# One ring of two-bank PSUM tiles, three score chunks a visit, and an exemption between readers of bank 0 and writers of bank 1

## The chip, the cores and the metric

One core of one Trainium2 chip. The metric is the device time of one execution in microseconds. Each comparison uses executions in the fast state only, timed on the same chip in the same rounds as the kernel before; an execution in the slow state (one of e1 below, at 629 us) is left out. The granted clock is the share of TensorE's full clock that the profile records as given to it. Each core has eight PSUM banks, the buffers that matmuls write and ScalarE and VectorE read.

## The reference

```python
scores = scale * np.matmul(q, k.transpose(0, 1, 3, 2)) - np.log(S)   # 8 batches, 12 heads, S=448, D=64
attn = 1.0 / (1.0 + np.exp(-scores))                                 # a sigmoid, no softmax
x = np.matmul(attn, v)            # -> (3584, 768)
g = x @ w_gate                    # 768 x 1536
out = (g * sigmoid(g) * (x @ w_val)) @ w_out                         # 1536 x 768
```

So there are two matrix chains: attention in 64-wide heads, and a gated feed-forward block with 128x128 matmuls.

## The kernel before

Attention works on 24 groups `n` of four heads, three groups to a batch. Each group has seven score "chunks" of four 64x64 matmuls, one sigmoid on ScalarE for a chunk, and a "pv" of 28 matmuls. The first batch's attention runs alone. All the later attention is woven into the feed-forward stream in **visits**: TensorE leaves its 128x128 matmuls, does two score chunks, sometimes a pv, and goes back.

```python
psA = ctx.enter_context(tc.tile_pool(name="psA", bufs=2, space=bass.MemoryType.PSUM))  # scores: 2 x 2 banks
psG = ctx.enter_context(tc.tile_pool(name="psG", bufs=4, space=bass.MemoryType.PSUM))  # the rest: 4 x 1 bank
...
def trans_pe(n, which):                      # q or k of one group
    t = q16.pop((n, which))
    ps = psG.tile([128, C, 128], BF16, tag="G", name="ps_tr")
    for c in range(C):
        nc.tensor.transpose(out=ps[:, c, :], in_=t[:, c].rearrange(...), identity=idn)
    d = qkT.tile([128, C, 128], BF16, tag=f"T{which}", ...)
    nc.vector.tensor_copy(out=d, in_=ps)
...
def ffn1(b, f, gate):                        # one gate or one value group
    ps = psG.tile([128, S], FP32, tag="G", name="ps_g" if gate else "ps_vl")
    for pr in range(NP):
        nc.tensor.matmul(out=ps, lhsT=w[:, pr, cs], rhs=xT[(b, pr)], ...)
    if gate:
        nc.scalar.activation(out=s16, in_=ps, func=SIGM)
        nc.vector.tensor_tensor(out=t1, in0=ps, in1=s16, op=MULT)
    else:
        nc.vector.scalar_tensor_tensor(out=hT[...], in0=ps, scalar=HSC, in1=gcur[0], op0=MULT, op1=MULT)
...
visits = [tiles[i:i + 2] for i in range(0, len(tiles), 2)]
def attn_step(group, pvs):
    scs = [(n, c, qk_tile(n, c)) for n, c in group]
    for n in pvs:
        pv(n)
    for n, c, sc in scs:
        sig_tile(n, c, sc)
```

## Time and profile before

| | before |
|---|---|
| time, median of 3 | 449.12 us (449.05 to 449.71) |
| span of the profiled execution | 446.4 us |
| TensorE busy | 420.9 us, 94% |
| VectorE, ScalarE busy | 49%, 47% |
| mean granted TensorE clock | 0.992 |

With one engine at 94% of the span, the first guess is that it bounds the kernel. The view that tests this is not the busy table but who made TensorE wait, and then where inside its stream time goes that isn't matmuls. The prediction below shows those lines.

### The profile page before, as it was taken

The page shows a single profiled execution, that of the slowest core. Times are in us where ns is not written, and L with a number is a line of the kernel's source. Part 1 is how long each engine was busy: PE and PEld are TensorE (multiplying, and loading weights), DVE is VectorE, ACT ScalarE, POOL GpSimd, SP SyncE. Part 2 cuts the span into 40 slices and gives each one's busy share as a digit, 9 for nine tenths or more (in the row PEclk, how much of TensorE's full clock was granted, in tenths as well). Part 3 has the DMA queues.
Part 4 walks back from the last instruction along what each step waited for, and adds up shares of the span by engine and source line. Part 5 has one row for each costly group of instructions (what it writes and reads, how often), then busy time and mean ns, then how long its engine had stood idle before and what let it go on. Part 6 is the DMA issues. An engine that isn't in the chain of part 4 may idle for free.

```text
span 446.4 us, 7870 instructions
## 1 busy us (share of the span) xinstructions
PE 420.9 (94%) x3252; PEld 212.2 (48%) x3252; DVE 220.1 (49%) x360; ACT 210.9 (47%) x267; POOL 100.7 (23%) x142
## 2 busy tenths in 40 slices
PE   2678999999999999999999999999999999999992
PEld 1344444444555444444555444444555545555661
DVE  1265665466334456556424546646524446555231
ACT  3887675655533655565444464565444441221000
POOL 1764140220234512000324612200021100000221
PEclk9899999999999999999999999999999999999998
DMA  8999999994284986500278694220033300000242
GB/s 264 332 286 286 182 249 196 232 280 149 58 249 94 262 248 167 164 1 1 50 222 231 135 302 134 42 42 3 0 82 87 79 4 1 1 1 0 72 106 70
DMA packets 63587, 59.88 MB, mean 134 GB/s; under 512 B 35648, under 2 KB 61760, under 8 KB 63552
## 3 DMA queue, kind: packets, MB, share of 16 engines
q1 hardware_dynamic: 52992, 41.30, 34.8%
q0 software_dynamic: 10560, 18.09, 19.3%
q8 instruction: 25, 0.41, 0.4%
q14 instruction: 10, 0.08, 0.1%
HBM read 47.19 MB, written 11.01 MB: 130 GB/s over the span
## 4 chain that ended last, share of the span: by engine, by line
PE 92%; ACT 2%; DMA 2%; DVE 1%; issue 1%; POOL 0%; SPq 0%; POOLq 0%; ACTq 0%
PE ps_o L213 25%; PE ps_vl L186 25%; PE ps_g L186 25%; PE ps_sc L137 9%; PE ps_pv L160 7%; ACT pt L148 2%; DMA st<-in_q_dram 2%; PE ps_tr L120 1%; DVE xT L170 1%; SPq L88 0%; POOL c L108 0%; DVE osb L220 0%; POOL out_dram L228 0%; POOLq L391 0%; ACTq L148 0%
## 5 line engine op out<-in xcount | busy, mean ns | idle before, releaser
L148 ACT ACTIVATE pt<-ps_sc,sb_t 128x896 f16<-128x896 f32 x168 | 159.6, 1005 | 88.5 <-PE ps_sc L137 88.5
L186 PE MATMUL ps_g<-xT,wg 128*128 128x448 f16 x576 | 125.4, 353 | 1.5 <-DVE xT L170 1.4
L186 PE MATMUL ps_vl<-xT,wv 128*128 128x448 f16 x576 | 124.9, 353 | 0.0
L213 PE MATMUL ps_o<-wo,hT 128*128 128x384 f16 x672 | 113.5, 326 | 0.0
L193 DVE TENSOR_TENSOR t<-ps_g,s 128x448 f16<-128x448 f32 x96 | 59.9, 624 | 84.7 <-ACT s L191 84.1
L191 ACT ACTIVATE s<-ps_g 128x448 f16<-128x448 f32 x96 | 52.2, 544 | 103.2 <-PE ps_g L186 103.2
L213 PEld LDWEIGHTS <-hT 128*128 128x128 f16 x672 | 64.0, 98 | 48.6 <-issue 7.9
L186 PEld LDWEIGHTS <-wv 128*128 128x128 f16 x576 | 54.3, 98 | 58.6 <-issue 10.7
L186 PEld LDWEIGHTS <-wg 128*128 128x128 f16 x576 | 54.1, 98 | 57.0 <-issue 9.7
L228 POOL DMA_DIRECT2D out_dram<-osb x56 | 29.3, 528 | 211.2 <-DVE osb L220 211.0
L170 DVE CAST xT<-ps_pv 64x448 f16<-64x448 f32 x96 | 59.7, 622 | 30.8 <-PE ps_pv L160 29.4
L198 DVE SCALAR_TENSOR_TENSOR hT<-ps_vl,t 128x448 f16<-128x448 f32 x96 | 60.0, 625 | 16.6 <-PE ps_vl L186 8.5
L220 DVE TENSOR_SCALAR osb<-ps_o 128x384 f32<-128x384 f32 x56 | 31.2, 558 | 74.6 <-PE ps_o L213 74.4
L137 PE MATMUL ps_sc<-T,T 64*64 64x448 bf16 x672 | 51.1, 370 | 8.8 <-ACT pt L148 7.2
L108 POOL CAST c<-st 128x896 bf16<-128x896 f32 x43 | 39.7, 939 | 54.7 <-DMA st<-in_q_dram 30.3
L108 POOL CAST v<-st 128x896 f16<-128x896 f32 x24 | 22.6, 942 | 72.8 <-PE ps_pv L160 52.9
L160 PE MATMUL ps_pv<-pt,v 64*64 64x448 f16 x672 | 37.5, 359 | 0.3 <-ACT pt L148 0.3
L137 PEld LDWEIGHTS <-T 64*64 64x64 bf16 x672 | 13.7, 106 | 39.7 <-issue 37.1
L160 PEld LDWEIGHTS <-v 64*64 64x64 f16 x672 | 20.8, 109 | 12.8 <-issue 0.9
L120 PE MATMUL ps_tr<-idn,c 128*128 128x128 bf16 x84 | 7.3, 250 | 6.5 <-DVE c L108 4.7
L120 PEld LDWEIGHTS <-c 128*128 128x128 bf16 x84 | 5.9, 113 | 8.8 <-DVE c L108 4.7
L124 DVE COPY T<-ps_tr 128x896 bf16<-128x896 bf16 x12 | 7.1, 620 | 5.4 <-PE ps_tr L120 5.2
(14 smaller groups left out, 17.2 us busy)
## 6 DMA issues: line engine op xcount, KB each, us to landing
st<-in_q_dram SPq DMA_DIRECT2D x24, 448.0 KB, 4.5
st<-in_k_dram SPq DMA_DIRECT2D x24, 448.0 KB, 5.9
st<-in_v_dram SPq DMA_DIRECT2D x24, 448.0 KB, 7.3
out_dram<-osb POOLq DMA_DIRECT2D x56, 192.0 KB, 3.1
wg<-in_moe_w_gate_dram POOLq DMA_DIRECT2D x4, 576.0 KB, 24.8
wv<-in_moe_w_val_dram POOLq DMA_DIRECT2D x4, 576.0 KB, 29.7
wo<-in_moe_w_out_dram POOLq DMA_DIRECT2D x4, 576.0 KB, 35.4
T<-c SPq DMA_TRANSPOSE x36, 3.2
```

The lines of the kernel that those rows point to most:

```text
L108: eng.tensor_copy(out=o, in_=i)
L137: nc.tensor.matmul(out=sc[w * 64:(w + 1) * 64, h2, :S], lhsT=kt[r, c, w * 64:(w + 1) * 64], rhs=qt[r, :, w * 64:(w + 1) * 64], start=True, ...
L148: nc.scalar.activation(out=pt, in_=sc[:, :, :S], func=SIGM, bias=sb_t, scale=qkscale)
L160: nc.tensor.matmul(out=P[w][h2 * 64:(h2 + 1) * 64, :], lhsT=vt[r, h2, c * D:(c + 1) * D], rhs=pt[r, h2, :], start=(c == 0), stop=(c == C - 1),
L170: nc.vector.tensor_copy(out=x[w * 64:(w + 1) * 64, :], in_=P[w][h2 * 64:(h2 + 1) * 64, :])
L186: nc.tensor.matmul(out=ps, lhsT=w[:, pr, cs], rhs=xT[(b, pr)], start=(pr == 0), stop=(pr == NP - 1))
L191: nc.scalar.activation(out=s16, in_=ps, func=SIGM)
L193: nc.vector.tensor_tensor(out=t1, in0=ps, in1=s16, op=MULT)
L198: nc.vector.scalar_tensor_tensor(out=hT[(b // 2, f)][:, b % 2, :], in0=ps, scalar=HSC, in1=gcur[0], op0=MULT, op1=MULT)
L213: nc.tensor.matmul(out=o, lhsT=lhsT, rhs=wo16[f // FW][:, f % FW, half * hw:(half + 1) * hw], start=(f == 0), stop=(f == NF - 1),)
L220: nc.vector.tensor_scalar(out=osb[:, half * hw:(half + 1) * hw], in0=o, scalar1=HREC, scalar2=None, op0=MULT)
L228: nc.gpsimd.dma_start(out=dst, in_=osb[i * 64:(i + 1) * 64, :])
```

## The change

The eight PSUM banks become one pool of four two-bank tiles that everything shares: a gate and its value group together ("G"), a score chunk, a pv, the transposes of q and k together, and an output pair. A visit takes three chunks, with the pv between the second and the third. The aim is fewer changes between the two forms of matmul, 128x128 and 64x64. Since gate and value now share a tile, the readers of the gate's bank are declared independent of the matmuls that write the value's bank: `declare_no_dep` tells the language that no wait is needed between them (an exemption). The output pair has the same for its first half.

```diff
-    psA = ctx.enter_context(tc.tile_pool(name="psA", bufs=2, space=bass.MemoryType.PSUM))
-    psG = ctx.enter_context(tc.tile_pool(name="psG", bufs=4, space=bass.MemoryType.PSUM))
+    psD = ctx.enter_context(tc.tile_pool(name="psD", bufs=4, space=bass.MemoryType.PSUM))
...
+    def trans_pe(n):
+        ps = psD.tile([128, 2, 8, 128], BF16, tag="D", name="ps_tr")
+        for which in range(2):
+            t = q16.pop((n, which))
+            for c in range(C):
+                nc.tensor.transpose(out=ps[:, which, c, :], ...)
+            d = qkT.tile([128, C, 128], BF16, tag=f"T{which}", name=f"T{which}_{n}")
+            nc.vector.tensor_copy(out=d, in_=ps[:, which, :C, :])
...
+    def ffn1(b, f):
+        D = psD.tile([128, 2, 512], FP32, tag="D", name="ps_gv")
+        key = f"bank1_{b}_{f}"
+        for i, w16 in enumerate((wg16, wv16)):
+            for pr in range(NP):
+                mm = nc.tensor.matmul(out=D[:, i, :S], ...)
+                if i == 1:
+                    tc.add_to_no_dep_group(key, mm.ins)
+        sg = nc.scalar.activation(out=s16, in_=D[:, 0, :S], func=SIGM)
+        tc.declare_no_dep(sg.ins, group=key, reason="reads bank 0; the group writes bank 1")
+        tm = nc.vector.tensor_tensor(out=t1, in0=D[:, 0, :S], in1=s16, op=MULT)
+        tc.declare_no_dep(tm.ins, group=key, reason="reads bank 0; the group writes bank 1")
+        nc.vector.scalar_tensor_tensor(out=hT[...], in0=D[:, 1, :S], scalar=HSC, in1=t1, ...)
...                                         # the output pair: the same, for its first half
-    visits = [tiles[i:i + 2] for i in range(0, len(tiles), 2)]
+    visits = [tiles[i:i + 3] for i in range(0, len(tiles), 3)]
...
-        scs = [(n, c, qk_tile(n, c)) for n, c in group]
+        scs = [(n, c, qk_tile(n, c)) for n, c in group[:2]]
         for n in pvs:
             pv(n)
+        scs += [(n, c, qk_tile(n, c)) for n, c in group[2:]]
```

## The prediction

> **What bounds the kernel now.** I read the page's busy shares first, then who waited for whom on TensorE, then the timeline of one stretch. The page:
>
> ```profile
> PE 420.9 (94%) x3252; PEld 212.2 (48%) x3252; DVE 220.1 (49%) x360; ACT 210.9 (47%) x267; POOL 100.7 (23%) x142
> ```
>
> TensorE is busy for 94% of the span; the next engine is at half. All waits of TensorE from 40 us to the end are these:
>
> ```profile
> core 0 of [0], span 446.4 us
> PE ps_g L186 <- DVE xT L170: 0.5, 1, 0.5
> ```
>
> One wait of half a microsecond in 406 us. So after the first 40 us the kernel is as long as its matmul stream, and a change of buffers can gain there only what lies inside that stream. The timeline of TensorE (start, duration, line, tile, count) shows what does:
>
> ```profile
> 203.27 0.57 PE L137 MATMUL ps_sc<-T,T 64*64 64x448 bf16 x8
> 203.67 1.49 PE L160 MATMUL ps_pv<-pt,v 64*64 64x448 f16 x28
> 205.10 1.31 PE L186 MATMUL ps_vl<-xT,wv 128*128 128x448 f16 x6
> 206.24 1.30 PE L186 MATMUL ps_g<-xT,wg 128*128 128x448 f16 x6
> ...
> 208.51 1.30 PE L186 MATMUL ps_g<-xT,wg 128*128 128x448 f16 x6
> 209.74 0.57 PE L137 MATMUL ps_sc<-T,T 64*64 64x448 bf16 x8
> 210.25 1.31 PE L186 MATMUL ps_vl<-xT,wv 128*128 128x448 f16 x6
> ```
>
> Durations overlap (the pipeline), so take start to start. Six 128x128 matmuls take 206.24 - 205.10 = 1.14 us. If score matmuls follow, they begin 209.74 - 208.51 = 1.23 us after, so going from the 128x128 to the 64x64 form costs about 0.095. Two score chunks before the attention-times-V matmuls ("pv") take 0.40, so 0.20 a chunk; before 128x128 matmuls they take 0.51, so going back costs 0.11. **One visit to the scores thus costs 0.205 us beside its work**, and pv takes 1.33 of work.
>
> The sum closes: 192 groups of six x 1.135 = 217.9; 56 output groups x 1.95 = 109.2; 147 chunks x 0.20 = 29.4; 21 pv x 1.33 = 27.9; 74 visits x 0.205 = 15.2; about 1.6 of transposes: 401 us. From the start of the steady stream at 37.2 to the end of the last matmul at 438.1 the timeline shows 401.
>
> The first 35 us are different. There ScalarE's 21 sigmoids of 0.9 us set the pace, and it is starved around each pv:
>
> ```profile
> 22.52 0.46 PE L137 MATMUL ps_sc<-T,T 64*64 64x448 bf16 x4
> 22.81 2.53 DVE L170 CAST xT<-ps_pv 64x448 f16<-64x448 f32 x4 [6.37 <-PE ps_pv L160]
> 22.91 0.95 PE L120 MATMUL ps_tr<-idn,c 128*128 128x128 bf16 x14
> 23.09 1.01 ACT L148 ACTIVATE pt<-ps_sc,sb_t 128x896 f16<-128x896 f32 x1 [1.76 <-PE ps_sc L137]
> ...
> 25.37 1.16 DVE L124 COPY T<-ps_tr 128x896 bf16<-128x896 bf16 x2
> ```
>
> Here the 14 transposes run while VectorE still casts pv's result; the two copies of them come after, and TensorE doesn't wait. The brackets of ScalarE's idle time between 11 and 35 us add up to 4 us.
>
> **What the Trainium skill says.** "TensorEngine Tiling (Array Packing)", Key Properties: "Mode switching requires drain". The 0.095 + 0.11 us above agrees. "PSUM — Partial Sum Buffer", PSUM bank collisions raise a hardware error: two engines collide only in the same bank and quadrant; different banks run clean. So reading bank 0 while bank 1 is written is sound; no run yet shows it here. "Trainium Kernel Development and Optimization", Best Practices: consistent bubbles can mean that SBUF or PSUM ran out. The kernel before has no such bubbles, and I expect them after.
>
> **The change part by part.**
>
> *Fewer visits.* 147 chunks in threes are 49 visits instead of 74. 25 x 0.205 = **-5.1 us**, all on TensorE's path. No matmul goes away: The counts of groups, chunks and pv stay the same in the new loops. ScalarE and VectorE do the same instructions.
>
> *The ring.* Before, a gate or value group took one of four single banks and scores had their own two pairs, so no group waited. Now a gate-and-value pair ("G", 2.27 us of matmuls), a chunk, a pv, a transpose tile and an output pair each take one of four slots in order, and each waits for the readers of the fourth before it. When three chunks lie between two G, **the second G waits for the first G's last reader**. How late is that? An undisturbed chain in the kernel before:
>
> ```profile
> 363.64 1.30 PE L186 MATMUL ps_g<-xT,wg 128*128 128x448 f16 x6
> 364.77 1.30 PE L186 MATMUL ps_vl<-xT,wv 128*128 128x448 f16 x6
> 364.97 0.54 ACT L191 ACTIVATE s<-ps_g 128x448 f16<-128x448 f32 x1 [1.25 <-PE ps_g L186]
> 365.55 0.62 DVE L193 TENSOR_TENSOR t<-ps_g,s 128x448 f16<-128x448 f32 x1 [1.08 <-ACT s L191]
> 366.27 0.62 DVE L198 SCALAR_TENSOR_TENSOR hT<-ps_vl,t 128x448 f16<-128x448 f32 x1
> ```
>
> The last reader ends 366.89 - 363.64 = 3.25 us after the start, and TensorE sees it some 0.06 later (the gap from the T copy to the first score matmul at 9.11): 3.31. TensorE is ready for the next G after 1.14 + 1.23 + 3 x 0.20 + 0.11 = 3.08. So each such place costs 0.24 us, more where ScalarE or VectorE is behind. I wrote out the order in which the new loops emit their work and counted: 18 visits without a pv stand between two G, and one between a G and a transpose tile, 19 places. 16 of them find the other engines free (their last pv is two G back, or the last visit three): 16 x 0.24 = 3.8. Two come two G after another pv-less visit, whose three sigmoids held up the gate sigmoid: 2 x 0.4 = 0.8. One comes a single G after a pv, whose casts hold VectorE for 2.5 us: 0.85. Together **+5.5 us**. Where a pv sits between the chunks nothing waits (the G is needed 1.0 us later), and an output pair's slot is free just in time (0.62 us after its matmuls against 0.71 of chunks). The exemption matters here: without it the sigmoid would start 1.1 us later, and each of these waits would grow.
>
> *The first G* now takes the slot of the last pv before it, so it cannot start five matmuls ahead of the casts: 5 x 0.19, less a hidden chunk, **+0.8**.
>
> *The first 35 us.* The scores may run three or four chunks ahead instead of two, so ScalarE starves less: I follow the slots through and get 1.6 us of gaps where 3.0 stood, and give some back since a pv holds a slot for 4 us: **-1**.
>
> *Transposes.* Both transposes of a pair now share a tile, and the copy of the first stands in the program ahead of the seven transposes of the second. No exemption is declared here. That one had to be declared for G suggests that dependencies are otherwise tracked for the tile as a whole; then the second seven wait for the first copy, and this copy queues behind pv's casts. In the first 35 us it delays the next score by about 2.1 us twice; in the stream there are two pairs left, one behind a free VectorE (0.45 of transposes, then a copy of 0.62 + 0.1: +0.75) and one right behind a pv (the casts end 4.5 us after the visit's start, the copy 5.1, the transposes are done at 2.5: +2.65). Together **+7.7 if tracked by tile, 0 if by bank**.
>
> Sum: -5.1 + 5.5 + 0.8 - 1 = +0.2, so 449.3 by bank; 449.3 + 7.7 = 457.0 by tile. I hold tracking by tile for 60% likely: 0.4 x 449.3 + 0.6 x 457.0 = 453.9, and I predict 454.
>
> **The rivals.** (1) *The gain stands.* If release were faster than I think, or the wait overlapped the drain at the change of form, the 19 bubbles vanish and 5 to 6 us remain: 443. For it: the margin is only 0.24 us of 3. Against: the chain above is the best case that the old kernel shows, at a moment with idle ScalarE and VectorE. (2) *The bubbles grow.* Three sigmoids in a row hold ScalarE 2.85 us instead of 1.9, and a gate sigmoid behind them would be up to 1.5 us late. For it: in the stretch from 35 to 100 us ScalarE is busy 42 of 65 us. Against: most pv-less visits come two or three G after the last visit, when ScalarE has caught up. If all 16 cheap places cost 0.5 instead of 0.24, the sum grows by 4: 453 to 461. (3) *The transposes cost nothing*, tracking by bank: 449.
>
> **Range and chances.** The two branches are 449 and 457; rival 1 takes some 3 off, rival 2 adds some 3 to 5. So 446 to 460. Faster by 2% needs 440, below even the full gain with nothing lost: 3%. Slower by 2% needs 458.1, which is only 1.1 over the second branch: 0.6 x 0.4 = 24%. The rest, 73%, is within 2%.
>
> **What would show it.** Right, if TensorE's waits after 40 us, one before, become some 18 to 20 of a G for VectorE's hT, 0.2 to 0.4 us each, only after visits of three bare chunks; if the change of form is paid 49 times with 0.2 each; and if transposes wait for a T copy, longest after a pv. Wrong, if G never waits (rival 1), if the waits are mostly over 0.6 us with ScalarE busy before them (rival 2), or if transposes run 14 in a row as now (branch by bank). A granted clock below 0.99, or a slower rate inside the groups of six, would be something that I haven't seen at all.

## The result, and the profile after

The changed kernel takes **454.16 us** (452.66 to 455.57, 4 runs) against 449.09 for the kernel before: ratio 1.011, 95% interval 1.0074 to 1.0146. It is correct, slower by about 5 us, and inside 2%. A ratio here is the mean time of one kernel's fast runs over that of the other's of the same rounds, so it is not quite the ratio of the medians.

The busy line of the page, to be read against the one of before:

```profile
PE 421.1 (93%) x3252; PEld 219.9 (49%) x3252; DVE 221.2 (49%) x360; ACT 210.3 (46%) x267; POOL 100.7 (22%) x142
```

The work is the same to 0.3 us on TensorE, but the span grew from 446.4 to 453.0. All waits of TensorE after 40 us (microseconds in total, times, longest):

```profile
PE ps_gv L188 <- DVE hT L202: 4.0, 18, 0.8
PE ps_tr L122 <- DVE T L126: 3.3, 2, 2.6
PE ps_tr L122 <- DVE hT L202: 0.2, 1, 0.2
PE ps_gv L188 <- DVE xT L172: 0.2, 1, 0.2
```

One wait became 22. Eighteen are of a gate for the last reader of a slot, and two are of the second seven transposes for the copy of the first seven. The timeline of TensorE shows what each gate wait costs in the path. First a visit between two G, then one between two output pairs, where nothing waits:

```profile
63.47 0.76 PE L139 MATMUL ps_sc<-T,T 64*64 64x448 bf16 x12
64.42 1.29 PE L188 MATMUL ps_gv<-xT,wg 128*128 128x448 f16 x6 [0.19 <-DVE hT L202]
...
122.03 0.76 PE L139 MATMUL ps_sc<-T,T 64*64 64x448 bf16 x12
122.75 4.06 PE L214 MATMUL ps_o<-wo,hT 128*128 128x384 f16 x24
```

From the first score matmul to the next 128x128 matmul it is 0.95 us with the wait and 0.72 without. The path cost is 0.23 us, a little more than the 0.19 of idle time in the bracket: without a wait the next matmul starts 0.04 us before the scores' recorded end (0.72 against 0.76), and that overlap is lost too. This is why start-to-start intervals are a better measure than the brackets.

The longest wait of a transpose, with the engines that take part:

```profile
56.20 0.56 PE L122 MATMUL ps_tr<-idn,c 128*128 128x128 bf16 x7
58.70 0.62 DVE L126 COPY T<-ps_tr 128x896 bf16<-128x896 bf16 x1
59.37 0.90 PE L122 MATMUL ps_tr<-idn,c 128*128 128x128 bf16 x7 [2.60 <-DVE T L126]
60.07 2.33 PE L188 MATMUL ps_gv<-xT,wg 128*128 128x448 f16 x6
62.24 1.30 PE L188 MATMUL ps_gv<-xT,wv 128*128 128x448 f16 x6
```

Fourteen transposes are split in two. The copy could start only at 58.70, when VectorE was through with pv's four casts, and TensorE stood still. Then the next gate group takes 62.24 - 60.07 = 2.17 us instead of 1.14: the granted clock from 59.4 to 62.3 us is 0.52. (A second profile of this kernel, e5 below, has the wait and not the lower clock.) The same split in the first 35 us starves ScalarE:

```profile
30.11 0.93 PE L122 MATMUL ps_tr<-idn,c 128*128 128x128 bf16 x7
30.29 1.01 ACT L150 ACTIVATE pt<-ps_sc,sb_t 128x896 f16<-128x896 f32 x1 [0.67 <-PE ps_sc L139]
32.41 0.62 DVE L126 COPY T<-ps_tr 128x896 bf16<-128x896 bf16 x1
33.09 0.55 PE L122 MATMUL ps_tr<-idn,c 128*128 128x128 bf16 x7 [2.05 <-DVE T L126]
34.07 2.80 ACT L150 ACTIVATE pt<-ps_sc,sb_t 128x896 f16<-128x896 f32 x3 [2.77 <-PE ps_sc L139]
```

To see where the loss lies, cut the run at two marks that both kernels have: the first output matmul, and the block of 168 output matmuls that closes the kernel. The rows are before's two marks, then the changed kernel's:

```profile
110.55 2.11 PE L213 MATMUL ps_o<-wo,hT 128*128 128x384 f16 x12
410.59 14.63 PE L213 MATMUL ps_o<-wo,hT 128*128 128x384 f16 x89
```

```profile
118.04 4.06 PE L214 MATMUL ps_o<-wo,hT 128*128 128x384 f16 x24
417.14 8.13 PE L214 MATMUL ps_o<-wo,hT 128*128 128x384 f16 x49
```

Between the marks the changed kernel is *faster*, 299.10 against 300.04 us. All of the loss, 7.5 us in these two executions, comes before the first mark.

### The profile page after: what moved, and what is told of

It is laid out like the page before. It is cut to its first block, busy times and chain, and to the rows that moved or that the text cites. A ratio compares the mean times of both kernels' runs of the same rounds, so it can differ in the third digit from the quotient of the medians.

```text
span 453.0 us, 7872 instructions
## 1 busy us (share of the span) xinstructions
PE 421.1 (93%) x3252; PEld 219.9 (49%) x3252; DVE 221.2 (49%) x360; ACT 210.3 (46%) x267; POOL 100.7 (22%) x142
## 4 chain that ended last, share of the span: by engine, by line
PE 82%; DVE 9%; ACT 4%; issue 1%; DMA 1%; POOL 0%; POOLq 0%; SPq 0%; DVEq 0%; ACTq 0%
PE ps_gv L188 44%; PE ps_o L214 24%; PE ps_pv L162 8%; PE ps_sc L139 5%; DVE hT L202 3%; DVE xT L172 3%; DVE t L198 3%; ACT s L195 2%; ACT pt L150 2%; PE ps_tr L122 1%; DMA st<-in_k_dram 1%; DVE T L126 1%; ACT L150 0%; ACT c L107 0%; DVE osb L224 0%
## 5 line engine op out<-in xcount | busy, mean ns | idle before, releaser
L150 ACT ACTIVATE pt<-ps_sc,sb_t 128x896 f16<-128x896 f32 x168 | 156.8, 1005 | 101.6 <-PE ps_sc L139 101.5
L188 PE MATMUL ps_gv<-xT,wg 128*128 128x448 f16 x576 | 125.9, 355 | 5.0 <-DVE hT L202 4.0
L188 PE MATMUL ps_gv<-xT,wv 128*128 128x448 f16 x576 | 124.6, 352 | 0.0
L214 PE MATMUL ps_o<-wo,hT 128*128 128x384 f16 x672 | 111.8, 326 | 0.0
L198 DVE TENSOR_TENSOR t<-ps_gv,s 128x448 f16<-128x448 f32 x96 | 60.0, 625 | 89.6 <-ACT s L195 88.0
L195 ACT ACTIVATE s<-ps_gv 128x448 f16<-128x448 f32 x96 | 52.3, 545 | 98.4 <-PE ps_gv L188 96.9
L188 PEld LDWEIGHTS <-wv 128*128 128x128 f16 x576 | 56.4, 98 | 53.2 <-issue 0.8
L202 DVE SCALAR_TENSOR_TENSOR hT<-ps_gv,t 128x448 f16<-128x448 f32 x96 | 60.0, 625 | 10.8 <-DVE t L198 0.5
L139 PE MATMUL ps_sc<-T,T 64*64 64x448 bf16 x672 | 49.7, 375 | 1.7 <-ACT pt L150 0.9
L109 POOL CAST c<-st 128x896 bf16<-128x896 f32 x43 | 39.9, 944 | 49.7 <-DMA st<-in_q_dram 23.8
L139 PEld LDWEIGHTS <-T 64*64 64x64 bf16 x672 | 15.9, 109 | 26.5 <-issue 20.3
L122 PE MATMUL ps_tr<-idn,c 128*128 128x128 bf16 x84 | 9.2, 270 | 15.1 <-DVE T L126 8.1
```

The lines of the kernel that those rows point to most:

```text
L109: eng.tensor_copy(out=o, in_=i)
L139: nc.tensor.matmul(out=sc[w * 64:(w + 1) * 64, h2, :S], lhsT=kt[r, c, w * 64:(w + 1) * 64], rhs=qt[r, :, w * 64:(w + 1) * 64], start=True, ...
L150: nc.scalar.activation(out=pt, in_=sc[:, :, :S], func=SIGM, bias=sb_t, scale=qkscale)
L188: mm = nc.tensor.matmul(out=D[:, i, :S], lhsT=w16[f // FW][:, pr, cs], rhs=xT[(b, pr)], start=(pr == 0), stop=(pr == NP - 1),)
L195: sg = nc.scalar.activation(out=s16, in_=D[:, 0, :S], func=SIGM)
L198: tm = nc.vector.tensor_tensor(out=t1, in0=D[:, 0, :S], in1=s16, op=MULT)
```

## The experiments

My theory is that of the prediction: the saved visits are taken back by the gate waits, and the shared transpose tile costs the rest. The rivals: the gate waits cost nothing, the exemption does nothing, or the transposes' waits are hidden. All runs gave correct results, and all ratios are to the kernel before on the same chip.

| run | what | median us | ratio, 95% interval |
|---|---|---|---|
| e1_tfix | transposes first, and exempted | 449.87 | 1.0016 (0.9973 to 1.0058) |
| e2_ring2 | change, two chunks a visit | 455.07 | 1.0136 (1.0093 to 1.0180) |
| e3_noexempt | change without exemptions | 472.13 | 1.0520 (1.0465 to 1.0576) |
| e4_before3 | before, three chunks a visit | 473.84 | 1.0558 (1.0505 to 1.0611) |
| e5_after_again | the change again | 454.50 | 1.0115 (1.0084 to 1.0146) |
| e6_tfix_again | e1 again | 447.60 | 0.9974 (0.9937 to 1.0011) |
| e7_persist | e1 with a hand-made ring | 449.54 | 1.0008 (0.9976 to 1.0040) |
| e8_exact | e7, gates wait for bank 0 only | 444.15 | 0.9891 (0.9848 to 0.9934) |
| e9_exact_again | e8 again | 445.19 | 0.9894 (0.9848 to 0.9940) |
| e10_exact2 | e9, two chunks a visit | 452.02 | 1.0040 (1.0001 to 1.0078) |
| e11_earlyw | e9, a weight block asked for earlier | 444.35 | 0.9879 (0.9838 to 0.9919) |
| e12_latewo | e11, output weights asked for later | 443.31 | 0.9886 (0.9844 to 0.9927) |

**Transposes ahead of both copies, and exempted (e1, e6).**

```diff
         for which in range(2):
             t = q16.pop((n, which))
             for c in range(C):
-                nc.tensor.transpose(out=ps[:, which, c, :], ...)
-            d = qkT.tile(...)
-            nc.vector.tensor_copy(out=d, in_=ps[:, which, :C, :])
+                mm = nc.tensor.transpose(out=ps[:, which, c, :], ...)
+                if which == 1:
+                    tc.add_to_no_dep_group(key, mm.ins)
+        for which in range(2):
+            d = qkT.tile(...)
+            cp = nc.vector.tensor_copy(out=d, in_=ps[:, which, :C, :])
+            if which == 0:
+                tc.declare_no_dep(cp.ins, group=key, reason="reads bank 0; the group writes bank 1")
```

> The change, with the 14 transposes of a pair emitted ahead of the two copies and the first copy exempted from the second seven. Theory (the shared transpose tile is tracked as a whole and costs the second seven a wait): TensorE's five waits for a T copy, 8.1 us together, vanish; ScalarE's two idle stretches of 2.8 us in the first 35 us shrink to under 1 us; the half-rate stretch that follows the 2.6 us wait at 57 us (about 1.4 us lost) goes with it. 454.2 - 4.2 - 3.3 - 1.4 = about 445.5, range 444 to 448. Rival (the waits were hidden behind ScalarE or given back by the ring): 451 or more.

The edit does two things. All 14 transposes now stand ahead of both copies, so that the second seven have no copy before them to wait for; and the first copy need not wait for the second seven. Neither was run alone.

Measured 449.87, half of the gain that I had expected, so a miss in size. All five waits for a T copy were gone. Its profiled execution had fallen into a slow state (629 us, granted clock 0.757), so it could not say where the rest went. I ran it again beside the changed kernel:

> The changed kernel once more, as the control for the three that follow on the same chip. Both theories: 1.011 times the kernel before, 453 to 455.5; TensorE waits 8 us for T copies and 4 us for hT.

> The first experiment again, since its profile fell into a slow state and its time (449.9) gave back only half of the 8.9 us that I expected. If the waits for the T copies were worth 8.9 and that chip's runs were unlucky: 445 to 447.5. If something takes the place of these waits (the first sigmoids, casts of the next inputs, a lower clock): 449 to 451, and the trace, in its fast state this time, has to show it: a longer first 40 us, new waits, or a half-rate stretch.

The changed kernel repeated its time (454.5), and e6 came to 447.6, 6.9 us less; its single runs spread from 446.4 to 450.6. The trace shows two things. In the first stretch ScalarE runs its 21 sigmoids without a gap:

```profile
9.93 18.98 ACT L156 ACTIVATE pt<-ps_sc,sb_t 128x896 f16<-128x896 f32 x21
32.17 1.30 PE L194 MATMUL ps_gv<-xT,wv 128*128 128x448 f16 x6
```

Between these sigmoids ScalarE idles 7.3 us in the changed kernel and 3.4 in the kernel before. The first value matmul comes 32.17 - 9.93 = 22.2 us after the first sigmoid, against 30.1 in the changed kernel (31.5 in e5) and 26.3 in the kernel before. After that, something takes the place of the waits:

```profile
44.17 1.31 PE L194 MATMUL ps_gv<-xT,wv 128*128 128x448 f16 x6 [2.03 <-DMA wv<-in_moe_w_val_dram]
45.32 2.36 PE L194 MATMUL ps_gv<-xT,wg 128*128 128x448 f16 x6
```

TensorE now reaches the second block of value weights before it has landed, waits 2.0 us, and then works at about half rate for a while (granted clock 0.67 from 44.2 to 49.4 us). From the first value matmul to the first output matmul e6 takes 78.0 us, no less than the changed kernel's 77.9, though its waits for T copies there (3.3 us) are gone. The theory holds: the waits for T copies cost 4.4 to 6.3 us of time by these two ratios (1.0115 less 1.0016, or less 0.9974), and part of what their removal saves is given back to a transfer. This profile is of one of the faster executions of e6 (446.83); whether the slower ones wait longer is not shown.

**Two chunks a visit in the ring (e2).**

```diff
-    visits = [tiles[i:i + 3] for i in range(0, len(tiles), 3)]
+    visits = [tiles[i:i + 2] for i in range(0, len(tiles), 2)]
```

> The change, but two chunks a visit as before (74 visits). Theory (the saved visits, 5.1 us, and the 19 waits of a gate for the last reader of the slot, 4.8 us in the path, cancel): no wait of a gate matmul for hT is left, the visits cost 5.1 more, sum 454.5 (453 to 456). Rival (the waits overlapped the change of form, so three chunks gained 5 us and the transposes cost more than I think): 459.

455.07 against an expected 454.5. No gate waits for hT any more, and the 25 added visits cost about as much as these waits did. Three chunks a visit gain nothing in this kernel that whole times can tell (ratios 1.0136 and 1.0110); between the two marks they gain 1.3 us (417.34 - 116.92 = 300.42 in e2, against 299.10).

**Without the exemptions (e3).** All `declare_no_dep` lines are taken out.

> The change without its exemptions (all other text equal). Theory: the gate sigmoid starts after the value matmuls, 1.14 us later, so the 18 waits of a gate grow from 0.2 to about 1.35 us (+20 us), the third chunk behind a pv waits some 0.35 us at about 13 places (+4.5), and an output pair's slot comes free 0.56 us later at 8 places (+4.5): 480 to 487. Rival (the dependencies are tracked by bank anyway and the exemption does nothing): 454.

472.13: the exemptions of G and of the output pair are together worth 18 us (1.0520 less 1.0115, of 449). My figure was too high by 8 to 15, and the trace tells why:

```profile
50.95 0.76 PE L139 MATMUL ps_sc<-T,T 64*64 64x448 bf16 x12
51.06 0.54 ACT L195 ACTIVATE s<-ps_gv 128x448 f16<-128x448 f32 x1 [2.38 <-PE ps_gv L188]
52.29 0.62 DVE L200 SCALAR_TENSOR_TENSOR hT<-ps_gv,t 128x448 f16<-128x448 f32 x1
52.55 1.29 PE L188 MATMUL ps_gv<-xT,wg 128*128 128x448 f16 x6 [0.84 <-ACT pt L150]
```

The sigmoid does start only after the value matmuls. But the next gate starts at 52.55 while hT, which reads the G before, runs until 52.91. So it does not use that slot: it waited for a chunk's sigmoid, 0.84 us (19 times, 15.6 in all) where I had expected 1.35. The third chunks behind a pv, for which I had counted 4.5 us, don't wait at all. The pool hands out its four slots not strictly in turn; here the gate got a chunk's slot, which came free sooner.

**Three chunks on the old buffers (e4).** `visits`, `attn_step` and the chunk after which the transposes are emitted (4 instead of 5) as in the change, everything else as before.

> The kernel before with three chunks a visit alone (scores keep their two slots, everything else its four banks). Theory: at the 29 visits without a pv the third chunk waits for the first sigmoid, 1.55 us after the visit's start instead of 0.40, so 29 x 1.15 = 33 us are lost against 5.1 gained: about 477 (470 to 482). Rival (ScalarE has slack to hide it): below 455.

473.84, inside the expected 470 to 482. TensorE's waits after 41 us:

```profile
PE ps_sc L137 <- ACT pt L148: 26.6, 28, 1.0
```

With two score slots the third chunk waits about 1 us for the first sigmoid at 28 visits. Three chunks a visit need more than these two score slots.

**Gates wait for their own bank only (e7, e8).** e7 keeps four tiles allocated and reuses them by hand in turn. e8 adds one exemption:

```diff
         old = readers1.pop(si, None)        # group of the slot's last reader of bank 1
...
                 if i == 1:
                     tc.add_to_no_dep_group(key, mm.ins)
+                elif old:
+                    tc.declare_no_dep(mm.ins, group=old, reason="writes bank 0; the group reads bank 1")
```

> As the run before it in this job, but the ring is four tiles that stay allocated and are reused by hand, without any new exemption: a control for the next run. Both theories: the time of that run within 1 us, with some 18 waits of a gate for hT.

> The ring by hand, and one more exemption: gate matmuls, which write bank 0, don't wait for the slot's last reader of bank 1 (hT); the value matmuls do. Theory (the wait of a gate is for the other bank's reader, and costs 4.3 to 4.8 us in the path): no gate waits for hT any more, a value group needs it 1.14 us later when it is long done, and the time falls by 4 to 5 us against the control. Rival (the waits lie under the change of form and the path is set by something else): within 1 us of the control.

The control e7 has its 18 waits and 449.54 us, which is 1.9 above e6's median, more than the 1 us that I had allowed. With slots strictly in turn some of its waits are longer: 5.9 us together, against 4.0 in the changed kernel. e8 has none and takes 444.15: 5.4 us less than the control, and 1.1% less than the kernel before. The stretch between the two marks shows it without the noise of the start. The rows are the marks of e7, then those of e8:

```profile
112.01 4.06 PE L236 MATMUL ps_D<-wo,hT 128*128 128x384 f16 x24
411.96 13.33 PE L236 MATMUL ps_D<-wo,hT 128*128 128x384 f16 x81
```

```profile
108.80 4.06 PE L238 MATMUL ps_D<-wo,hT 128*128 128x384 f16 x24
404.46 20.80 PE L238 MATMUL ps_D<-wo,hT 128*128 128x384 f16 x127
```

It is 295.66 us against 299.95: the one added exemption is worth 4.29 us there. The 12 gate waits that e7 has in this stretch add up to 3.69 in the brackets, and 12 x 0.04 of lost overlap makes 4.2. The changed kernel takes 299.10, 3.44 more than e8, and has 12 gate waits there too, 11 short ones and the long one of 0.76: 11 x 0.24 + 0.8 = 3.4. The gate waits are thus the whole difference in both pairs. e9, e11 and e12 below repeat the 295.66 to 0.01.

**What a visit costs by itself (e9, e10).** The edit of e2, on e8.

> The hand-made ring with both exemptions again, as the control for the next two on the same chip: 0.989 times the kernel before, single runs from 442 to 447.

> As the control, but two chunks a visit (74 visits). Theory (a visit costs 0.205 us of TensorE beside its work, and now nothing takes it back): 25 x 0.205 = 5.1 us slower than the control. Rival (the first 40 us or the wait for weights set the difference): within 1.5 us of the control. No gate waits for hT in either.

e9 repeated e8 (445.19). e10 took 6.8 us more (452.02), where I had expected 5.1. Its marks:

```profile
114.07 4.06 PE L238 MATMUL ps_D<-wo,hT 128*128 128x384 f16 x24
414.49 10.73 PE L238 MATMUL ps_D<-wo,hT 128*128 128x384 f16 x65
```

300.42 us between the marks, 4.76 more than e8. The emission order has 55 visits there against 36 and one more chunk: 19 x 0.205 + 0.20 = 4.1, and 0.4 is a wait of an output matmul, which three chunks a visit don't have: 4.5. So the cost of a visit holds to 0.3 us over 19 (0.22 a visit instead of 0.205). The rest of the 6.8 lies before the mark, with waits for xT (1.4 us) and for weights.

**The scatter of the last version (e11, e12).** e8 and e9 have single runs from 441.8 to 447.6. e11 moves the two `w_load` calls of block 1 up, before the third pair's casts. e12 also holds back the output weights (`if wl and n >= 5`).

> As the control, but the second block of gate and value weights is asked for some 3 to 4 us earlier, ahead of the casts of the third pair. Theory (since TensorE reaches this block earlier, it waits for it in some executions, and 2 us of wait bring a half-rate stretch with 1.8 us more): the slow ones of the executions go, the runs lie at 441.5 to 443.5, and no wait for these weights is in the profile. Rival (the block is late because the transfers share what they can move, and asking earlier only delays the inputs beside it): same scatter as the control, or slower by the sigmoids of the first 35 us.

> The run before with the four output-weight transfers asked for some 25 us later (with the visits of the sixth and seventh head group instead of the fourth and fifth), so that they don't share with the gate and value weights that TensorE is about to need; they have until about 115 us. Theory (what is left of the scatter is the wait of value matmuls for their weights, up to 2.5 us each with a stretch at half rate behind it, because the transfers share what they can move): no wait for these weights, runs at 440.5 to 443 without a second cluster at 445, ratio to the kernel before about 0.983. Rival (the transfers that hold them up are the next inputs, or the scatter has another cause): runs between 441 and 446 as before, or a new wait of output matmuls for their weights.

Neither did what I expected. e11's wait for block 1 was gone in its profile, but waits for value weights of later blocks stood in its place (3.6 us in two), and its runs still spread from 441.1 to 445.9. e12's profile has one:

```profile
68.61 1.31 PE L207 MATMUL ps_D<-xT,wv 128*128 128x448 f16 x6 [2.62 <-DMA wv<-in_moe_w_val_dram]
```

That is for the last of the four blocks, and its runs spread from 442.4 to 446.4. So the waits for weights are real and move from block to block, but holding back the output weights does not end them. Inputs of later head groups are asked for in the same stretch (from 49.7 to 52.3 us in e12); whether these hold the weights up is open, and so is how much of the scatter the waits explain.

## Why the prediction was right

The time is 454.16 against 454 predicted, in the range, and "within 2%" had most of the chance. That the middle fits so well is partly luck: 454 was a weighted mean of two branches, 449.3 and 457.0. The branch "tracked by tile" came true, and its own sum is 3 us too high; inside it, two errors of about 4 us in the first stretch cancel. By its steps:

- **What bounds the kernel: right.** TensorE's work did not change; the difference lies in waits, changes of form and a short stretch at a lower clock.
- **Fewer visits, -5.1: right.** e10 against e8 gives 4.8 us for 19 visits, one chunk and a wait of 0.4, which leaves 0.22 a visit.
- **The ring, +5.5 at 19 places: right in kind and number.** There are 18 waits of a gate and one of a transpose; each common one costs 0.23 to 0.24 in the path. The one expected at 0.85 stands at 0.76. The two places put at 0.4 cost no more than the others. With the brackets' 4.0 + 0.2 us and some 0.04 a place of lost overlap, the term is about 5.0. e8 against e7 gives 5.4, for e7's longer waits.
- **Transposes, +7.7 if tracked by tile: the mechanism and the long waits right, what they are worth wrong.** (Its parts add up to 7.6.) In the stream, 0.75 and 2.65 were predicted, 0.71 and 2.60 measured. In the first 35 us, 2.1 twice was predicted, and the waits are 2.05 twice; a third of 0.71, at 12.70 us, was not counted. ScalarE idles 2.77 us behind each of the two long ones, and without the three waits e6 gets through this stretch about 7.9 us sooner (30.1 - 22.2), where the step had 4.2. Yet in the whole time only 4.4 to 6.3 us come back, since TensorE then meets weights that have not landed. The prediction had no step for that.
- **The first 35 us and the first G, -1 and +0.8: wrong, and only the sum of the stretch is right, by luck.** From the first sigmoid to the first value matmul it is 37.43 - 11.10 = 26.3 us before and 40.14 - 10.02 = 30.1 after, +3.8; the steps for this stretch give -1 + 0.8 + 4.2 = +4.0. But e6, which has the ring and not the waits for T copies, takes 22.2 here in its one fast profile: the ring gains about 4.1 us where -0.2 stood, which hides that the waits cost about 7.9 and not 4.2. ScalarE's gaps between the 21 sigmoids, of which the prediction left 1.6 us, are gone in e6. Nor did the first G take the last pv's slot: it waited 0.8 us for a chunk's sigmoid. The hand-made ring, where slots go strictly in turn, has the wait that I described (2.1 us for the casts in e8). The first sigmoid itself came 1.1 us earlier, with an input that landed earlier, which no step had.
- **Not foreseen: the granted clock.** Half rate after the 2.6 us wait costs 2.17 - 1.14 = 1.0 us in one gate group. The prediction named a lower clock only as something that it had not seen.
- **Rival 1 (the gain stands)** falls by e2 and e8, **rival 2 (bubbles over 0.6 us)** by the 18 waits (17 of 0.19 and one of 0.76), and **rival 3 (tracking by bank)** by the five waits for T copies in the changed kernel.

From the two profiles, the balance before the first output matmul (+7.5): +2.7 up to the first value matmul, +3.5 for the transposes' waits in the stream (0.71, 2.60 and 0.19 for hT), about +1.4 for the half rate behind them, 6 gate waits x 0.24 = +1.4 against 6 visits fewer x 0.205 = -1.2, and -0.5 for a wait for xT that is gone: 7.3.

## What to carry to other kernels

When tiles were merged here to share buffers, the new tile was released by its *last* reader and, unless told otherwise, waited for as a whole (18 us in e3). So write down for each user who reads last, how late, and how many tiles later the slot comes round. A margin of a few tenths of a microsecond, read from start-to-start intervals of the old trace, was enough here to predict where the ring would stall, and the gain from fewer changes of form was kept only once those stalls were exempted. Exempt every pair that the banks make independent, not just the one that one thought of: the version with the transposes and the gates exempted too (444.2 us) beats both kernels by 1 and 2%, while the change without these was 1% slower than what it replaced. And check each stage of a prediction by itself: a right total can hide two wrong terms, as in the first stretch here.

## What the Trainium skill lacked or had wrong

- "TensorEngine Tiling (Array Packing)", Key Properties, says that a change of tiling mode drains TensorE but gives no cost. Here a visit from 128x128 to 64x64 and back costs 0.205 us (0.095 in, 0.11 out) by the intervals of the kernel before.
- "TensorE: Matmul & The Clock Gate", HAM oscillation, warns of TensorE idle gaps over some 3.4 us. Here the clock was low after shorter waits: 2.60 us in the changed kernel (granted 0.52 from 59.4 to 62.3 us; with the transposes around this wait, 3.9 us pass without another matmul), 2.03 us in e6 (0.67 from 44.2 to 49.4 us) and 2.06 us in e8 (0.57 from 34.2 to 38.2 us). The length of the wait does not decide it alone: after 2.61 us in e5, 2.06 us in e9 and 2.62 us in e12 the full rate stands.
- "PSUM — Partial Sum Buffer", PSUM bank collisions raise a hardware error: that one bank may be read while another is written is borne out: in the changed kernel the first gate sigmoid starts to read bank 0 at 40.33 us, while the value matmuls that began at 40.14 us write bank 1 for 1.30 us, and all runs with exemptions gave correct results. The page guards by bank and quadrant; it does not say that a tile of two banks may be guarded as one by the language's own tracking. That guard costs 18 us for G and the output pair (e3), and 4.4 to 6.3 us for the transposes, whose order e1 and e6 changed too.
- No page that I used says that a pool's slots need not be handed out in turn; e3's trace shows a gate that took a slot other than the fourth before it.
